# Splitting the first pair's input during the early attention steps, and resuming attention five slots later

## The chip, the cores and the metric

The kernel runs on one core of one Trainium2 chip. The metric is the device time of one execution in microseconds (us), the median of several runs. Profiles come from one profiled execution.

## What is computed

Three stages follow each other: attention against pooled keys and values, a mixture of eight experts with all experts used (weights balanced by eight rounds of row and column scaling), and a softplus network. All is float32; x has 2304 tokens of 512 channels.

```python
# attention: q, k, v are (4, 8, 576, 64); keys and values are means of 8 neighbours
k_p = k.reshape(B, H, Sp, 8, D).mean(axis=3)
v_p = v.reshape(B, H, Sp, 8, D).mean(axis=3)
x = softmax(q @ k_p.T / sqrt(D)) @ v_p          # -> (2304, 512)
# experts
P = exp(x @ w_gate - max)
for _ in range(8):
    P /= P.sum(1); P /= P.sum(0); P *= N / E
x = sum(P[:, e] * (relu(x @ w1[e]) @ w2[e]) for e in range(8))
# softplus network
out = softplus(x @ w_in) @ w_out
```

## The kernel before, in words

**The large products.** The tokens are cut into three pairs of token blocks (512, 896 and 896 tokens). For each pair, the expert stage runs 32 sets; a set is 256 hidden units of one expert. Each float32 operand is split into a high and a low part (`hi` is a copy to fp32r on ScalarE, `lo` the difference from it), and a product is three matmuls, hi·hi, hi·lo and lo·hi, for each of two pieces of 128 rows. The first layer of a set (`first_moe`) multiplies two 2 x 2 block matrices with seven products instead of eight: each takes one part of the weights (`A11`, `A12`, `A22` and the sums `S1` to `S4`, made by `sums_w1` on GpSimd and split by `prep_w1`) and one part of x: the blocks `b11`, `b21`, `b22` themselves, and the differences `t1` to `t4`. The differences for pair 0 are made by `t_sums` (line 437) and all seven parts are split by `splits` and `split_x` (lines 448 and 452), on VectorE or, for the numbers in `on_pool`, on GpSimd. TensorE takes the products in the order b11, t2, t1, t4, t3, b21, b22. Between them VectorE adds the results in PSUM (line 586): `u1` after t2 (t3, which accumulates onto the same bank, waits for it), and three sums after t3 (b22, the last product, waits for the second of them). Then come relu and split (lines 521 and 522) and the second layer (`second`: four token tiles for pair 0, tile `py`, added up on VectorE in line 658). The last product (`rest`) is issued behind the first tile of the second layer of the set before.

**The order is written by hand.** Each engine executes its instructions in the order of the program text. After each of the seven products and each of the four second-layer tiles the program calls `hook`, one slot; so a set of pair 0 has 11 slots (7 in the first set, since no second layer runs beside it).

**Attention** has 32 steps, each for 288 queries of a pair of heads. `attn_step(m)` issues: the transpose of the next queries (`channels_first`, TensorE `pq`, ScalarE `qT`), the scores of step m (`softmax`, TensorE `s`, VectorE line 317 and 318), the gate product every fourth step (`pg`), the transposes of the block before (`turn_attn`, `pa`, `aT`), keys for a pooled pair (`keys_first`, `pk`, `kbd`), the exponential (ScalarE line 321), its division (VectorE lines 325 to 327, GpSimd line 328), the product with the values (`mix`, `px`, which writes x), and at some steps the pooling of a pair of heads (`pool_kv`: two reductions on VectorE, lines 269 and 275; on GpSimd for the first four values). Which steps pool is set by the table `pool_at`: 0, 1, 3, 5, 7, 9, 11, 13 and so on to 25. Each needs its keys one step later (`turn_at`). The first ten steps (`AHEAD`) run alone, one after another, at the start. The others run inside slots: `hook` issues one in every fifth slot (2, 7, 12, ...), so step m stands in slot 2 + 5(m - 10), and steps 10 and 11 lie beside the first set.

**After attention** `finish_attention` puts further work into the list `side`, of which each slot takes one entry: the balancing of the weights, then `shares_to_raw` (line 814 on VectorE), which multiplies the results of the first experts of pair 0, kept unweighted until then, by their shares and adds them up.

Of the kernel before, what the change touches and what calls it, by code (L numbers as in the profile page):

```python
# [9 lines left out]
F32 = mybir.dt.float32  # L10
# [9 lines left out]
def attention_moe_softplus_kernel(  # L20
# [20 lines left out]
    HP = H // 2  # L41
    w_in = w_in.bitcast(U32)
    w_out = w_out.bitcast(U32)
    P = 128
# [18 lines left out]
    TP0 = PAIRS[0]  # L63
# [53 lines left out]
    def x_of(pair):  # L117
        return g_t[0][:, :KC * PAIRS[pair]].rearrange("p (c n) -> p c n", c=KC)
# [25 lines left out]
    raw_t = {}  # L144
# [3 lines left out]
    def load_w(which, n):  # L148
        if n >= len(sets):
            return  # L150
        _, kind, _, u = sets[n]
        shape = [P, KC, US] if which == 1 else [P, UC, DM]
        if kind == "moe":
            e, o = divmod(u, UPE)
            o *= US
            src = w1[e][:, o:o + US] if which == 1 else w2[e][o:o + US, :]
            src = src.rearrange("(c p) f -> p c f", p=P)
        else:
            src = (v1 if which == 1 else v2)[u]
        t = rpool.tile(shape, F32, tag=f"w{which}raw", name=f"w{which}raw")  # L160
        nc.sync.dma_start(t, src)
        raw_t[which, n] = t
# [65 lines left out]
    AHEAD = 10  # L228
# [5 lines left out]
    to_turn = []  # L234
# [30 lines left out]
    def pool_kv(i):  # L265
        kt, vt, pool = kv_t.pop(i)
        kp = at_p.tile([SP, 2, D], F32, tag="kp", name="kp", bufs=1)
        vp = at_p.tile([SP, 2, D], F32, tag="vp", name="vp", bufs=NK + 1)
        nc.vector.tensor_reduce(kp, kt.rearrange("p h t d -> p h d t"), axis=AX.X, op=ALU.add)
        if i < HP:  # L270
            pool_add(vt[:, :, 0:4, :], vt[:, :, 0:4, :], vt[:, :, 4:8, :])
            pool_add(vt[:, :, 0:2, :], vt[:, :, 0:2, :], vt[:, :, 2:4, :])
            pool_add(vp, vt[:, :, 0, :], vt[:, :, 1, :])
        else:
            nc.vector.tensor_reduce(vp, vt.rearrange("p h t d -> p h d t"), axis=AX.X, op=ALU.add)
        pooled[i] = kp, vp

        if pool is ld_p or next_kv[0] < 2 * HP:
            load_kv(pool)
# [25 lines left out]
    def softmax(m):  # L305

        ps = bank("s")
        qT = q_t.pop(m)
        kb = kbd[kv_of(m) % NK]
        for j in range(JH):  # L310
            nc.tensor.matmul(ps[:QP, j * 2 * SP:(j + 1) * 2 * SP], qT[:, j * QP:(j + 1) * QP], kb)
        sv = ps[:QP, :G * SP].rearrange("p (g s) -> p g s", g=G)
        pool = at_e if m < AHEAD and m % 3 == 2 else at_p
        mx = at_p.tile([QP, G], F32, tag="mx", name="mx")
        ex = pool.tile([QP, G, SP], F32, tag="ex", name="ex")
        s1 = ps[:QP, G * SP:G * SP + G]
        nc.vector.tensor_reduce(mx, sv, axis=AX.X, op=ALU.max)
        nc.vector.tensor_tensor(ex, sv, mx.unsqueeze(2).to_broadcast([QP, G, SP]), op=ALU.subtract)

        def exp():  # L320
            nc.scalar.activation(ex, ex, AF.Exp)

        def divide():
            sm = at_p.tile([QP, G], F32, tag="sm", name="sm")
            nc.vector.tensor_reduce(s1, ex, axis=AX.X, op=ALU.add)
            nc.vector.tensor_scalar_add(s1, s1, 1e-9)
            nc.vector.reciprocal(sm, s1)
            nc.gpsimd.tensor_tensor(ex, ex, sm.unsqueeze(2).to_broadcast([QP, G, SP]), op=ALU.mult)
            to_turn.append((m, ex))

        return exp, divide

    def turn_attn():
        m, ex = to_turn.pop(0)
        aT = at_p.tile([SP, 2, W], F32, tag="aT", name="aT")
        for h in range(2):
            pa = bank("pa")
            for j in range(JH):
                nc.tensor.transpose(pa[:SP, j * QP:(j + 1) * QP], ex[:, 2 * j + h, :], ident[:QP, :QP])
            nc.scalar.copy(aT[:, h, :], pa[:SP, :W])  # L340
        to_mix.append((m, aT))
# [40 lines left out]
    pool_at = {}  # L382
    for i in range(2, B * HP):
        b, hp = divmod(i, HP)
        pool_at.setdefault(hp - 2 if b == 0 else 2 * HP * b - 5 + 2 * hp, []).append(i)
    turn_at = {}
    for m, l in pool_at.items():
        turn_at.setdefault(m + 1, []).extend(l)
    turn_at.setdefault(0, []).append(1)

    def attn_step(m, early):


        last = STEPS
        if m + 1 < last:
            channels_first(m + 1)
        if m < last:
            exp, divide = softmax(m)
        while to_gate:
            gate()  # L400
        while to_turn:
            turn_attn()
        for i in turn_at.get(m, ()):
            keys_first(i)
        if m < last:
            exp()
            to_divide.append(divide)
        while len(to_divide) > (1 if early else 0):
            to_divide.pop(0)()
        while len(to_mix) > (0 if early or m >= last else 1):  # L410
            mix()
        for i in pool_at.get(m, ()):
            pool_kv(i)

    for i, pool in enumerate((ld_e, ld_e, ld_p, ld_p)):
        load_kv(pool)
# [18 lines left out]
    def t_sums(x, t, on_pool=()):  # L435

        sub = lambda i, o, a, b: (nc.gpsimd if i in on_pool else nc.vector).tensor_tensor(o, a, b, op=ALU.subtract)
        return [
            lambda: sub(0, t(0), block(x, 0, 1), block(x, 0, 0)),
            lambda: sub(2, t(2), block(x, 1, 1), block(x, 0, 1)),  # L440
            lambda: sub(1, t(1), block(x, 1, 1), t(0)),
            lambda: sub(3, t(3), block(x, 1, 0), t(1)),
        ]
# [41 lines left out]
    def splits(kind, x, t, on_pool=(), pair=None):  # L485
        if kind == "moe":
            l = moe_parts(x, t)
        else:
            l = [
                (f"c{c}{j}", x[:, c:c + cs, j * tb:(j + 1) * tb])  # L490
                for cs, tb in (sp_parts(x.shape[2]),) for j in range(x.shape[2] // tb) for c in range(0, KC, cs)
            ]
        return [
            lambda i=i, a=a: split_x(*a, i in on_pool, None if pair is None else xlod[pair][:, i])
            for i, a in enumerate(l)
        ]
# [284 lines left out]
    def hook(light=True):  # L781
        slot[0] += 1
        if attn_m[0] is not None:
            if slot[0] % 5 == 2:
                attn_step(attn_m[0], False)
                attn_m[0] += 1
                if attn_m[0] >= STEPS and not to_turn and not to_mix and not to_gate:
                    attn_m[0] = None
                    finish_attention()
        elif side:  # L790
            x = side.pop(0)
            if x is not None:
                x()
        elif converting[0] is not None and light and "c" in banks:
            converting[0] += 1
            if converting[0] % 3 and next(conversion, 0) == 0:
                converting[0] = None
# [7 lines left out]
    def shares_to_raw(experts):  # L805

        for e in experts:
            for i in range(TP0 // P):
                def add(i=i, e=e):
                    a, s = acc_of(1, i), prob[:, i, e:e + 1]  # L810
                    if e == 0:
                        nc.scalar.activation(a, a, AF.Copy, scale=s)
                    else:
                        nc.vector.scalar_tensor_tensor(a, raw_of(e, i), s, a, op0=ALU.mult, op1=ALU.add)  # L814
                side.extend([add, None, None] if e else [add])

    def load_x(pair):
        o = OFF[pair] - TP0
# [2 lines left out]
    def t_in(g, pair):  # L821
        v = g_t[g][:, :KC * PAIRS[pair]].rearrange("p (q c n) -> p q c n", q=4, c=2)
        return lambda i: v[:, i]


    for m in range(AHEAD):
        attn_step(m, True)
        if m == 4:
            sums_w1(0)
        if m == 6:  # L830
            prep_w1(0)
            load_w(1, 1)
    ectx.close()
    hctx = ExitStack()
    hpool = hctx.enter_context(tc.tile_pool(name="h", bufs=2, side="right"))
    zpool = hctx.enter_context(tc.tile_pool(name="z", bufs=2, side="right"))
    tpool = None


    ta = hpool.tile([P, 2, 2, TP0 // 2], F32, tag="hhi", name="ta")  # L840
    tb = hpool.tile([P, 2, 2, TP0 // 2], F32, tag="hlo", name="tb")
    t0_of = lambda i: (ta, tb)[i // 2][:, i % 2]
    first_sums = t_sums(x_of(0), t0_of, on_pool=(2,))
    first_splits = splits("moe", x_of(0), t0_of, on_pool=(2, 4))
    first_sums[0]()
    first_splits[0]()
    for x in first_sums[1:]:
        x()
    for x in first_splits[1:]:
        x()  # L850


# [24 lines left out]
    for step, (what, n) in enumerate(todo):  # L877
# [4 lines left out]
        elif what == "first":  # L882
            f, kind, pair, u = sets[n]
            nxt = sets[n + 1] if n + 1 < len(sets) else None
            if not n or sets[n - 1][0] != f:
                xs.update(xs_next)
                xs_next.clear()
            if nxt is not None and nxt[1] == "moe":
                sums_w1(n + 1)
            if nxt is not None and nxt[0] != f:  # L890

# [114 lines left out]
```

## Time and profile before

| | before |
|---|---|
| runs | 2066.97, 2070.39, 2071.49 us; median 2070.39 |
| profiled execution | 2070.89 us, its span 2069.1 us |
| TensorE busy | 2020.9 us, 98% |
| VectorE, ScalarE, GpSimd busy | 1446.9, 829.4, 1242.5 us |
| TensorE's mean granted clock | 0.990 |

The rows further down are of the profiled execution, in us from the start of its span. PE is TensorE, DVE VectorE, ACT ScalarE, POOL GpSimd. A row of a timeline is one instruction or a run of equal ones: start, duration, engine, line, what it writes and reads; in brackets the idle time of the engine before it and what ended that. PEclk is the clock that TensorE was granted as a share of full speed: 0.50 is the lower of its two levels (1.2 GHz), 1.00 the upper (2.4 GHz).

### The profile page before, as it was taken

How to read it: one execution, taken by the hardware profiler on the slowest of the kernel's cores; microseconds unless marked ns; L12 is line 12 of the kernel's file. 1: busy time of each engine (PE TensorE's matmuls, PEld its weight loads, DVE VectorE, ACT ScalarE, POOL GpSimd, SP SyncE). 2: the span in 40 equal slices, each digit the busy share in tenths (PEclk: the TensorE clock that was granted, in tenths of full speed). 3: DMA queues.
4: the chain of work that ended last, by engine and by line, in shares of the span. 5: the costliest groups of instructions: out<-in, count | busy, mean ns of one | idle time of the engine just before them, and what ended most of it. 6: DMA issues, size and time to landing. Idle time of an engine off the chain costs nothing.

```text
span 2069.1 us, 27593 instructions
## 1 busy us (share of the span) xinstructions
PE 2020.9 (98%) x10285; PEld 1745.6 (84%) x10285; DVE 1446.9 (70%) x2467; ACT 829.4 (40%) x1567; POOL 1242.5 (60%) x995
## 2 busy tenths in 40 slices
PE   7899999999999999999999999999999999999998
PEld 5677888888888888888888888888888888888887
DVE  7787587776677777767776776777655666767756
ACT  4555544354322332222243223222222365565554
POOL 4666689987566645556565555665555554544555
PEclk9799999999999999999999999999999999999999
DMA  6343223444223332222242222222211111121132
GB/s 183 87 142 108 87 92 107 149 145 165 85 92 109 93 102 82 90 92 82 87 152 84 72 87 77 92 88 76 74 54 62 62 53 50 62 87 52 62 117 72
DMA packets 133762, 192.00 MB, mean 93 GB/s; under 512 B 26924, under 2 KB 82940, under 8 KB 133628
## 3 DMA queue, kind: packets, MB, share of 16 engines
q1 hardware_dynamic: 133628, 190.25, 29.3%
q8 instruction: 80, 1.31, 0.3%
q14 instruction: 54, 0.44, 0.1%
HBM read 166.94 MB, written 23.27 MB: 92 GB/s over the span
## 4 chain that ended last, share of the span: by engine, by line
PE 80%; POOL 3%; DVE 2%; ACT 1%; DMA 1%; issue 1%; POOLq 0%; SPq 0%; DVEq 0%; ACTq 0%
PE py L506 41%; PE p L506 29%; PE ph L506 9%; POOL w1lo L168 1%; POOL w2lo L168 1%; DMA xlod<-xl 1%; DMA g<-xd 0%; PE pt L668 0%; ACT xhi L448 0%; DVE g L814 0%; ACT w1hi L199 0%; POOL sums L168 0%; DMA f<-in_moe_w_in_dram 0%; DVE g L662 0%; DVE c L537 0%
## 5 line engine op out<-in xcount | busy, mean ns | idle before, releaser
L506 PE MATMUL py<-w2hi,hhi 128*128 128x512 f32 x1440 | 567.6, 394 | 6.1 <-DVE g L662 3.3
L506 PE MATMUL py<-w2hi,hlo 128*128 128x512 f32 x1440 | 562.9, 391 | 0.8 <-POOL hlo L549 0.8
L506 PE MATMUL py<-w2lo,hhi 128*128 128x512 f32 x1440 | 562.4, 391 | 0.0
L168 POOL TENSOR_TENSOR w1lo<-w1raw,w1hi 128x512 fp32r<-128x512 f32 (+1 forms) x216 | 254.0, 1194 | 476.4 <-ACT w1hi L199 375.8
L506 PE MATMUL p<-xhi,w1hi 128*128 128x448 f32 (+1 forms) x1344 | 459.9, 342 | 12.1 <-DVE p L586 4.3
L506 PE MATMUL p<-xhi,w1lo 128*128 128x448 f32 (+1 forms) x1344 | 456.7, 340 | 4.6 <-POOL w1lo L168 4.6
L506 PE MATMUL p<-xlo,w1hi 128*128 128x448 f32 (+1 forms) x1344 | 457.0, 340 | 2.8 <-DVE xlo L452 2.6
L662 DVE SCALAR_TENSOR_TENSOR g<-py,prob,g 128x512 f32<-128x512 f32 x482 | 360.5, 749 | 99.7 <-PE py L506 87.6
L521 ACT ACTIVATE hhi<-p 128x448 fp32r<-128x448 f32 (+1 forms) x384 | 180.1, 494 | 422.8 <-PE p L506 407.5
L506 PEld LDWEIGHTS py<-w2hi,hhi 128*128 128x128 f32 x1440 | 271.1, 188 | 66.4 <-DVE g L662 4.0
L506 PEld LDWEIGHTS py<-w2hi,hlo 128*128 128x128 f32 x1440 | 271.0, 188 | 60.8 <-POOL hlo L549 1.7
L168 POOL TENSOR_TENSOR w2lo<-w2raw,w2hi 128x1024 fp32r<-128x1024 f32 x120 | 288.8, 2406 | 49.6 <-ACT w2hi L212 44.4
L506 PEld LDWEIGHTS py<-w2lo,hhi 128*128 128x128 f32 x1440 | 271.2, 188 | 50.1
L506 PEld LDWEIGHTS p<-xhi,w1hi 128*128 128x128 f32 x1344 | 256.1, 191 | 42.1 <-DVE p L586 5.8
L506 PEld LDWEIGHTS p<-xlo,w1hi 128*128 128x128 f32 x1344 | 256.1, 191 | 21.9 <-DVE xlo L452 3.4
L506 PEld LDWEIGHTS p<-xhi,w1lo 128*128 128x128 f32 x1344 | 256.2, 191 | 18.7 <-POOL w1lo L168 5.9
L588 ACT COPY za<-p 128x448 f32<-128x448 f32 (+1 forms) x96 | 46.0, 479 | 492.4 <-PE p L506 488.1
L168 POOL TENSOR_TENSOR w1lo<-sums,w1hi 128x1024 fp32r<-128x1024 f32 x96 | 231.9, 2416 | 0.0
L522 DVE SCALAR_TENSOR_TENSOR hlo<-p,hhi 128x448 fp32r<-128x448 f32 (+1 forms) x384 | 210.3, 549 | 25.1 <-ACT hhi L521 24.4
L586 DVE TENSOR_TENSOR za<-p,za 128x448 f32<-128x448 f32 (+1 forms) x96 | 53.4, 556 | 166.1 <-PE p L506 166.1
L549 POOL TENSOR_TENSOR hlo<-ln,hhi 128x448 fp32r<-128x448 f32 (+1 forms) x80 | 97.2, 1217 | 51.5 <-ACT hhi L548 51.2
L212 ACT CAST w2hi<-w2raw 128x1024 fp32r<-128x1024 f32 x120 | 126.2, 1052 | 0.0
(124 smaller groups left out, 2618.2 us busy)
## 6 DMA issues: line engine op xcount, KB each, us to landing
w1raw<-in_moe_w_dram SPq DMA_DIRECT2D x96, 512.0 KB
w2raw<-in_moe_w_dram SPq DMA_DIRECT2D x96, 512.0 KB
w1raw<-v SPq DMA_DIRECT2D x24, 512.0 KB
w2raw<-v SPq DMA_DIRECT2D x24, 512.0 KB
f<-in_moe_w_in_dram SPq DMA_DIRECT2D x16, 512.0 KB
v<-dt SPq DMA_DIRECT2D x32, 256.0 KB
f<-in_moe_w_out_dram SPq DMA_DIRECT2D x16, 512.0 KB
xlod<-xl SPq DMA_DIRECT2D x28, 224.0 KB
```

What stands on the lines that cost most here:

```text
L168: nc.gpsimd.tensor_tensor(o, a, b, op=ALU.subtract)
L212: nc.scalar.copy(hi, raw)
L506: nc.tensor.matmul(ps, lhs[a], rhs[b], start=first and i == 0, stop=last and i == 2, skip_group_check=goes_on,)
L521: nc.scalar.activation(hh, src, AF.Relu)
L522: nc.vector.scalar_tensor_tensor(hl, src, 0.0, hh.bitcast(F32), op0=ALU.max, op1=ALU.subtract)
L549: nc.gpsimd.tensor_tensor(hl, l, hh.bitcast(F32), op=ALU.subtract)
L586: add = lambda o, x, y: nc.vector.tensor_tensor(o, x, y, op=ALU.add)
L588: nc.scalar.copy(a, pa)
L662: nc.vector.scalar_tensor_tensor(a, py, prob[:, t, e:e + 1], a, op0=ALU.mult, op1=ALU.add)
```

## The change

Four parts:

1. The parts of pair 0 are made in the early steps where they can be: `b11` is split after step 6, `b21` after step 7, `t1` made and split after step 8; the other three differences and four splits come after step 9, in another order. Three of the subtractions (b11, t1, b21) and that of t3 go to GpSimd (before: t1 and t3). The differences lie in `g1` instead of in tiles of the `h` pool. The split of the first set's weights, and the load of the second set's, come after step 5 instead of 6, the sums of the second set's weights after step 8.
2. The pooling that stood in step 9 (the fourth pair of heads of its batch) moves to step 10, and its keys get a slot of their own.
3. Step 10 runs in slot 7 instead of 2, so step m stands in slot 2 + 5(m - 9). It first turns the block that is waiting.
4. `shares_to_raw` takes two slots for each addition instead of three; the buffers `ex` of steps 1, 4, 7 instead of 2, 5, 8 lie in the early pool.

```diff
-        pool = at_e if m < AHEAD and m % 3 == 2 else at_p
+        pool = at_e if m < AHEAD and m % 3 == 1 else at_p
@@ the table of pooling steps
-        pool_at.setdefault(hp - 2 if b == 0 else 2 * HP * b - 5 + 2 * hp, []).append(i)
+        at = hp - 2 if b == 0 else 2 * HP * b - 5 + 2 * hp
+        pool_at.setdefault(AHEAD if at == AHEAD - 1 else at, []).append(i)
+
+    to_key = []
     turn_at = {}
     for m, l in pool_at.items():
-        turn_at.setdefault(m + 1, []).extend(l)
+        if m != AHEAD:
+            turn_at.setdefault(m + 1, []).extend(l)
@@ attn_step
+        if m == AHEAD:
+            while to_turn:
+                turn_attn()
...
         for i in pool_at.get(m, ()):
             pool_kv(i)
+            if m == AHEAD:
+                to_key.append(i)
@@ hook
-            if slot[0] % 5 == 2:
+            if to_key and slot[0] % 5 == 1:
+                keys_first(to_key.pop(0))
+            if slot[0] > 5 and slot[0] % 5 == 2:
                 attn_step(attn_m[0], False)
@@ shares_to_raw
-                side.extend([add, None, None] if e else [add])
+                side.extend([add, None] if e else [add])
@@ the early steps
+    t0_of = t_in(1, 0)
+    sum1, sum3, sum2, sum4 = t_sums(x_of(0), t0_of, on_pool=(2,))
+    split_b11, split_t2, split_t1, split_t4, split_t3, split_b21, split_b22 = splits(
+        "moe", x_of(0), t0_of, on_pool=(0, 2, 4, 5)
+    )
     for m in range(AHEAD):
         attn_step(m, True)
         if m == 4:
             sums_w1(0)
-        if m == 6:
+        if m == 5:
             prep_w1(0)
             load_w(1, 1)
+        if m == 6:
+            split_b11()
+        if m == 7:
+            split_b21()
+        if m == 8:
+            sum1()
+            split_t1()
+            sums_w1(1)
...
-    ta = hpool.tile([P, 2, 2, TP0 // 2], F32, tag="hhi", name="ta")
-    tb = hpool.tile([P, 2, 2, TP0 // 2], F32, tag="hlo", name="tb")
-    t0_of = lambda i: (ta, tb)[i // 2][:, i % 2]
-    first_sums = t_sums(x_of(0), t0_of, on_pool=(2,))
-    first_splits = splits("moe", x_of(0), t0_of, on_pool=(2, 4))
-    first_sums[0]()
-    first_splits[0]()
-    for x in first_sums[1:]:
-        x()
-    for x in first_splits[1:]:
+    for x in (sum2, split_t2, sum3, sum4, split_t4, split_t3, split_b22):
         x()
@@ the first layer of a set
-            if nxt is not None and nxt[1] == "moe":
+            if nxt is not None and nxt[1] == "moe" and ("s", n + 1) not in raw_t:
                 sums_w1(n + 1)
```

The lines of VectorE's and GpSimd's instructions below are nine higher in the changed kernel where they lie behind the new ones (586 is 595, 658 is 667, 452 is 461, 437 is 446).

**VectorE, the attention step in slot 22** (the fourth slot of the third set), before: step 14. `p_1135` is the bank of t2 and t3, `p_1136` that of t1 and b22.

```order
L317 TENSOR_REDUCE mx<-s 96x6
L318 TENSOR_TENSOR ex<-s,mx 96x432
L299 TENSOR_SCALAR kbd_130<-pk 64x72 x2
L325 TENSOR_REDUCE s<-ex 96x6
L326 TENSOR_SCALAR s<-s 96x6
L327 RECIPROCAL sm<-s 96x6
L586 TENSOR_TENSOR za<-p_1135,za 128x256
L586 TENSOR_TENSOR p_1135<-p_1136,za 128x256
L586 TENSOR_TENSOR p_1137<-p_1137,za 128x256
L522 SCALAR_TENSOR_TENSOR hlo<-p_1134,hhi 128x256
L658 TENSOR_TENSOR g_93<-py,g_93 128x512
L586 TENSOR_TENSOR p_1136<-p_1136,u_1139 128x256
```

The same slot with the change: step 13.

```order
L317 TENSOR_REDUCE mx<-s 96x6
L318 TENSOR_TENSOR ex<-s,mx 96x432
L325 TENSOR_REDUCE s<-ex 96x6
L326 TENSOR_SCALAR s<-s 96x6
L327 RECIPROCAL sm<-s 96x6
L269 TENSOR_REDUCE kp<-kt 72x128
L275 TENSOR_REDUCE vp<-vt 72x128
L595 TENSOR_TENSOR za<-p_1086,za 128x256
L595 TENSOR_TENSOR p_1086<-p_1087,za 128x256
L595 TENSOR_TENSOR p_1088<-p_1088,za 128x256
```

The two reductions of the pooling stand between the softmax and the three sums; before, the slot had a key copy (`kbd`) and no pooling.

**VectorE, the attention step in slot 52** (the first slot of a set), before: step 20.

```order
L317 TENSOR_REDUCE mx<-s 96x6
L318 TENSOR_TENSOR ex<-s,mx 96x432
L299 TENSOR_SCALAR kbd_128<-pk 64x72 x2
L325 TENSOR_REDUCE s<-ex 96x6
L326 TENSOR_SCALAR s<-s 96x6
L327 RECIPROCAL sm<-s 96x6
L586 TENSOR_TENSOR u_1803<-p_1799,za 128x256
L586 TENSOR_TENSOR za<-p_1799,za 128x256
```

The same slot with the change: step 19.

```order
L317 TENSOR_REDUCE mx<-s 96x6
L318 TENSOR_TENSOR ex<-s,mx 96x432
L325 TENSOR_REDUCE s<-ex 96x6
L326 TENSOR_SCALAR s<-s 96x6
L327 RECIPROCAL sm<-s 96x6
L269 TENSOR_REDUCE kp<-kt 72x128
L275 TENSOR_REDUCE vp<-vt 72x128
L595 TENSOR_TENSOR u_1755<-p_1751,za 128x256
L595 TENSOR_TENSOR za<-p_1751,za 128x256
```

Here the reductions stand ahead of `u`.

**GpSimd, from the products of the early steps to the weight sums of the second set**, before (`g_92` holds x, `ta` and `tb` the differences):

```order
L328 TENSOR_TENSOR ex<-ex,sm 96x432 x3
L437 TENSOR_TENSOR tb<-g_92 128x512
L452 TENSOR_TENSOR xlo<-ta,xhi 128x512
L452 TENSOR_TENSOR xlo<-tb,xhi 128x512
L165 TENSOR_TENSOR sums<-w1raw 128x256
L168 TENSOR_TENSOR sums<-w1raw 128x256
L168 TENSOR_TENSOR sums<-sums,w1raw 128x256
L168 TENSOR_TENSOR sums<-w1raw,sums 128x256
```

With the change (`g_93` holds the differences), steps 6 to 9:

```order
L328 TENSOR_TENSOR ex<-ex,sm 96x432
L461 TENSOR_TENSOR xlo<-g_92,xhi 128x512
L328 TENSOR_TENSOR ex<-ex,sm 96x432
L461 TENSOR_TENSOR xlo<-g_92,xhi 128x512
L328 TENSOR_TENSOR ex<-ex,sm 96x432
L461 TENSOR_TENSOR xlo<-g_93,xhi 128x512
L165 TENSOR_TENSOR sums<-w1raw 128x256
L168 TENSOR_TENSOR sums<-w1raw 128x256
L168 TENSOR_TENSOR sums<-sums,w1raw 128x256
L168 TENSOR_TENSOR sums<-w1raw,sums 128x256
L328 TENSOR_TENSOR ex<-ex,sm 96x432
L446 TENSOR_TENSOR g_93<-g_92 128x512
```

A subtraction for x now stands behind each of three products, and the weight sums ahead of the product of step 8.

## Rows read from the trace of the kernel before

**Rows 1.** Page, section 1 (busy time, share, instructions) and section 2 (tenths in 40 slices).

```profile
PE 2020.9 (98%) x10285; PEld 1745.6 (84%) x10285; DVE 1446.9 (70%) x2467; ACT 829.4 (40%) x1567; POOL 1242.5 (60%) x995
...
PEclk9799999999999999999999999999999999999999
```

**Rows 2.** Timeline of TensorE, 48 to 86 us (start us, us, instruction, idle before and releaser).

```profile
48.31 0.74 PE L288 MATMUL pq<-ident,qt 96*128 96x96 f32 x3
...
51.51 1.65 PE L349 MATMUL px<-aT,vp 72*64 72x288 f32 x4
...
57.63 0.58 PE L506 MATMUL p<-xlo,w1hi 128*128 128x256 f32 x1 [2.64 <-DVE xlo L452]
58.01 0.41 PE L506 MATMUL p<-xhi,w1lo 128*128 128x256 f32 x1
58.22 0.41 PE L506 MATMUL p<-xhi,w1hi 128*128 128x256 f32 x1
...
70.09 0.41 PE L288 MATMUL pq<-ident,qt 96*128 96x96 f32 x3
70.34 0.90 PE L311 MATMUL s<-kbd,qT 128*96 128x144 f32 x6
...
74.23 0.39 PE L506 MATMUL p<-xhi,w1hi 128*128 128x256 f32 x1
...
80.75 0.58 PE L506 MATMUL p<-xhi,w1lo 128*128 128x256 f32 x1 [1.38 <-POOL w1lo L168]
...
85.62 0.68 PE L288 MATMUL pq<-ident,qt 96*128 96x96 f32 x3
```

**Rows 3.** Timelines of ScalarE, VectorE and GpSimd, 48 to 64 us.

```profile
53.20 0.36 ACT L357 ACTIVATE g<-px 128x224 f32<-128x224 f32 x1 [0.76 <-PE px L349]
...
53.74 0.62 ACT L448 CAST xhi<-g 128x512 fp32r<-128x512 f32 x1
...
56.30 0.67 DVE L437 TENSOR_TENSOR ta<-g 128x512 f32<-128x512 f32 x1
...
61.19 2.90 DVE L452 TENSOR_TENSOR xlo<-g,xhi 128x512 fp32r<-128x512 f32 x2
...
48.42 0.91 POOL L328 TENSOR_TENSOR ex<-ex,sm 96x432 f32<-96x432 f32 x1 [2.98 <-PE px L349]
```

**Rows 4.** Stretches: us, busy (x) of PE, PEld, DVE, ACT, POOL, PEclk, DMA share, GB/s.

```profile
41.50:53.00 11.50, 10.73 (x43) 7.07 (x43) 8.51 (x16) 5.39 (x14) 4.89 (x6) 0.53 0.51 137
58.00:69.30 11.30, 9.92 (x78) 8.80 (x77) 9.34 (x17) 5.80 (x15) 7.93 (x8) 0.65 0.13 38
77.70:86.00 8.30, 6.89 (x31) 6.60 (x32) 3.62 (x8) 1.37 (x5) 7.37 (x6) 0.50 0.67 199
195.00:200.00 5.00, 5.00 (x31) 4.14 (x35) 2.91 (x8) 2.03 (x4) 3.15 (x2) 0.66 0.24 85
```

**Rows 5.** Timelines of TensorE, then VectorE, step 25 (slot 77), 186 to 195 us.

```profile
186.30 0.41 PE L288 MATMUL pq<-ident,qt 96*128 96x96 f32 x3
...
188.51 0.39 PE L506 MATMUL p<-xhi,w1hi 128*128 128x256 f32 x1
...
190.03 0.40 PE L506 MATMUL py<-w2hi,hhi 128*128 128x512 f32 x1
...
195.00 0.38 PE L506 MATMUL p<-xhi,w1hi 128*128 128x256 f32 x1 [3.42 <-DVE p L586]
...
190.38 1.97 DVE L269 TENSOR_REDUCE kp<-kt 72x128 f32<-72x1024 f32 x1
192.27 1.88 DVE L275 TENSOR_REDUCE vp<-vt 72x128 f32<-72x1024 f32 x1
194.07 0.41 DVE L586 TENSOR_TENSOR za<-p,za 128x256 f32<-128x256 f32 x1
```

**Rows 6.** Timeline of TensorE, step 20 (slot 52).

```profile
154.06 0.39 PE L506 MATMUL p<-xhi,w1hi 128*128 128x256 f32 x1 [1.08 <-DVE u L586]
```

**Rows 7.** Instructions of line 814: duration ns min/median/max, first and last start us.

```profile
L814 DVE SCALAR_TENSOR_TENSOR g<-g,prob,g x13: 740/1255/2445, 322.5 to 370.4; 128x512 f32<-128x512 f32 x13
```

## The prediction

> **What bounds the kernel now.** I read the page first. TensorE is busy for 2020.9 of 2069.1 us [rows 1], so nearly all that can be won is in the 48 us where it waits, and in stretches where it runs at its lower level. The strip of its clock is below 9 in the second of 40 slices alone (51.7 to 103 us), and all that the change moves lies in the first 20% of the span. Next I read TensorE's timeline there. The last early attention step ends at 51.51 + 1.65 = 53.2 us; then TensorE waits, 2.64 us of it for one low half of x [rows 2], because the sums and splits of x begin only now: VectorE's first difference starts at 56.30, after the two reductions of a pooled pair [rows 3]. Later, the first two sets wait for low halves of weights; the last of these waits ends at 80.75, and the slot in which attention step 12 stands starts at 85.62 [rows 2]. The granted clock was 0.53, 0.65 and 0.50 in three stretches of these 45 us [rows 4]. Third, I looked for waits while attention runs beside the first pair, since the change moves all those steps. One stands out: 3.42 us before 195.00, for a sum of VectorE [rows 5].
>
> That wait is the key to the change. Step 25 starts on TensorE at 186.30. VectorE gets its softmax, then the two reductions that pool a pair: 190.38 to about 194.1. Behind them in its queue stand the three sums that the last product of the set needs (`rest`, on `b22`). TensorE has only `t3`, `b21` and one tile of the second layer to do meanwhile [rows 5]. Step 20 shows the same in small without pooling: a wait of 1.08 us for `u1` [rows 6].
>
> **The slots.** A set of pair 0 has 11 slots: k = 0 to 6 in its products, then 4 between the second layer's tiles. A step comes every 5 slots, a pooling step every 10, so the place of pooling in the set goes back by one with each. Counted from the program, before: steps 13, 15, ..., 25 pool at slots 17, 27, ..., 77, which are second-layer places 2, 1, 0, then k = 6, 5, 4, 3. Only the last, step 25 at k = 3, stands where sums follow closely. Five slots later, the same steps pool at slots 22, 32, 42, 52, 62, 72, 82: k = 3, 2, 1, 0, then second-layer places 3, 2, 1. The steps that don't pool take the harmless places. The order of the instructions agrees: pooling now stands directly ahead of the sums in steps 13, 15 and 17, and ahead of `u1` in 19 and 21.
>
> **Price of the pooling steps.** Take step 25 as the pattern (no gate, nothing left over from before) [rows 5]. From the start of a step to its end TensorE works 188.51 - 186.30 = 2.2 us, a product is (190.03 - 188.51)/2 = 0.76 with the first one's restart, say 0.72; the sum that `rest` needs comes 195.00 - 186.30 = 8.7 us after the step's start, `u1` (which would stand where `za` does at 194.07) about 8.2 us after it.
> - Step 13 (k = 3): the place of step 25, so 3.4 us.
> - Step 15 (k = 2): one product more as cover: 3.4 - 0.7 = 2.7 us.
> - Step 17 (k = 1): after its four products step 18 follows before `rest`, another 1.6 us and more of cover: no wait.
> - Step 19 (k = 0): TensorE needs `u1` after 2.2 + 3 x 0.72 = 4.4 us, and gets it at 8.2: 3.8 us.
> - Step 21 (last tile's place): four products, 2.2 + 2.9 = 5.1 us: 3.1 us.
> - Steps 23 and 25 have a tile or two and another step ahead of `u1`: no wait, as with 13 and 15 before.
>
> That is 13.0 us of new waits. Gone are the 3.42 us (slot 77 now holds step 24, which doesn't pool) and the 1.08 us (slot 52 is counted anew above): net **+8.5 us**. Bounds: +5 if each cover is 0.9 us longer than I count, and +9.6 if the 1.08 us comes on top.
>
> **The clock.** After the 3.42 us the granted clock over 195 to 200 was 0.66 [rows 4], which is 5 x 0.34 = 1.7 us lost; after 1.08 us nothing fell. Four waits of 2.7 to 3.8 us, all nearer to 3.42 than to 1.08, instead of one: 3 x 1.7 = **+5.1 us**; bounds 0 and 5.1. The Trainium skill, TensorE: Matmul & The Clock Gate, section HAM oscillation — how this bites in real kernels, speaks against the change in this way too: a wait ahead of every block of matmuls brings the lower level back each time. [...]
>
> **The early part.** Before, from 53.2 to 85.62 is 32.4 us, of which attention step 11 takes 74.23 - 70.09 = 4.1 [rows 2]; it is now done a step later, at the same price. So 28.3 us are to be compared. After, `b11` is split long before, and the pair's pooling (3.8 us on VectorE) no longer stands in front. TensorE starts at 53.2. At the low level a product is 6 x 0.21 = 1.3 us, from the steps of its matmuls [rows 2]. `t2` needs the last channels of x (copied by 53.56), a difference (0.67), a cast (0.62) and a subtraction, as long as the difference [rows 3], so 55.5; one of them may be held up by GpSimd, which costs 0.78: two subtractions took 2.90 instead of 1.34 beside it [rows 3]. `t2` then ends at 56.3 + 1.1 = 57.4. `t1`, `t4`, `t3`, `b21` follow without a wait: 2.9 us at full clock, 5.1 at half. Step 10 up to the end of its scores: 3.2 us at half clock (48.31 to 51.51 are the same pieces of step 9), some 1.6 at full [rows 2]. So the scores end between 61.9 and 65.7. From there the old chain holds, since the change leaves it: softmax, the copy and cast behind it, then the low halves of the second set's weights on GpSimd, which stand behind that step's product. In step 11 the scores ended at 70.34 + 0.90 = 71.2 and the last weight wait at 80.75: 9.5 us. Then 4.9 us to the slot of step 12. After: 76.3 to 80.1, or 23.1 to 26.9 us against 28.3: a gain of 1.4 to 5.2. Step 11 turned two blocks of attention ahead of that chain, step 10 turns one, so I take a value in the upper half, **-4 us**. Bounds: 0 (all five of VectorE's operations held up), and -8 with the low stretch 77.7 to 86 (8.3 us at 0.50, worth half of its 6.89 busy us [rows 4]) gone too.
>
> **What I cost at nothing.** The three splits, three subtractions of some 1.3 us and the second set's weight sums, now on GpSimd between steps 6 and 9: GpSimd idled for 2.98 us ahead of its product in step 8 [rows 3], and that of step 9 is needed in step 10 only. If that cover is gone, each of the three steps is 1.3 us longer. The weight load that comes one step sooner: its data are used 10 us later. Keys later by a step: one transpose in its own slot. The expert adds after attention, one in two slots instead of three: 13 of them took 740 to 2445 ns, median 1255 [rows 7], so 12 of them in 24 slots keep VectorE full for two sets; TensorE waited for none of them before. Bounds -1 and +3, taken as 0.
>
> **Sum.** -4 + 8.5 + 5.1 = +9.6 us. The profiled execution took 2070.9 us (span 2069.1), 0.5 above the median 2070.4; on the median this gives **2080 us**.
>
> **The rivals.**
> - *Operations of VectorE blocked throughout the start.* GpSimd's queue is now full from step 8 on (a subtraction, four weight sums, a product, a difference, a subtraction), and VectorE's five operations run beside it. 5 x 0.78 = 3.9 us eat the early gain: 2070.9 + 13.6 = 2084.5. The Trainium skill, SBUF — State Buffer, section Who interferes with whom, has this as a rule: a VectorE operation with two inputs in SBUF waits for a GpSimd one that reads SBUF, for its whole length. The 2.90 us agree. For it: the rows. Against it: VectorE got its turn between two operations of GpSimd there, so a wait is a part of one of these and not the row. Chance 0.2. In this case the change does not do what it says: x is split early, but not ready early.
> - *No difference.* The start gains the bound of 8, and the waits bring no lower clock: 2070.9 - 8 + 8.5 = 2071.4. For it: the weight waits and 8.3 us at 0.50 are there to be won. Against it: these hang on the attention step ahead, which stays. Chance 0.14.
> - *Faster: the clock stays up.* Starting without the gap of 53 to 58, TensorE would hold full clock from 41 us on. It decides if the granted clock is 1.00 through steps 8 and 9 as well. Worth half of the low share: 10.73 x 0.47 + 9.92 x 0.35 + 6.89 x 0.50 = 12.0 us [rows 4], and 4 us of waits; with 8.5 of new waits and no lower clock after them: 2070.9 - 16 + 8.5 = 2063.4. For it: in 58 to 69.3 us the clock was partly back already, 0.65 on the mean. Against it: in 41 to 53 TensorE was busy for 10.73 of 11.5 us and still had 0.53. Chance 0.16.
> - My forecast: 0.5.
>
> **How the numbers follow.** A measurement of this kernel can tell about 0.2%, 4 us, from no change. The forecast and the first rival are slower by more (0.7), the second is the same (0.14), the third faster (0.16). The range goes from the third rival's edge, 2064, to the first with the expert adds' upper bound, 2088. The likeliest case alone: 2075 to 2084.
>
> **What would show it.** Right: waits of 2.5 to 4 us on TensorE for the sums or `u1` in steps 13, 15, 19 and 21, none at 24, a low clock after each; `b11` without a wait right after the last early step, a first wait of at most 3 us for `t2`; two weight waits after step 10. Wrong: none of the four waits (then VectorE was ahead, and the time is below 2070), or full clock from 58 to 90 us.

## The result, and the profile after

The changed kernel takes **2083.15 us** (median of 4 runs, 2080.80 to 2086.52); the kernel before, on the same chip, 2070.66 us. The ratio is 1.0060, with a 95% interval of 1.0048 to 1.0073: slower by 10 to 15 us. The forecast was 2080, slower.

The page of the kernel after, sections 1 and 2, the rows that answer to [rows 1]:

```profile
PE 2019.4 (97%) x10285; PEld 1746.3 (84%) x10285; DVE 1449.2 (70%) x2465; ACT 829.8 (40%) x1567; POOL 1245.3 (60%) x997
...
PEclk9899999999999999999999999999999999999999
```

TensorE is no busier than before and the strip of its clock is a tenth better in one slice: whole-span rows don't show where 12 us went. The waits do. These are the waits of over 2 us in TensorE's timeline of the kernel after, 100 to 190 us, and VectorE's timeline ahead of the first of them:

```profile
105.65 0.58 PE L515 MATMUL p<-xhi,w1hi 128*128 128x256 f32 x1 [3.42 <-DVE p L595]
127.16 0.39 PE L515 MATMUL p<-xhi,w1hi 128*128 128x256 f32 x1 [2.75 <-DVE p L595]
161.69 0.39 PE L515 MATMUL p<-xhi,w1hi 128*128 128x256 f32 x1 [3.54 <-DVE u L595]
181.89 0.38 PE L515 MATMUL p<-xhi,w1hi 128*128 128x256 f32 x1 [2.86 <-DVE u L595]
...
100.92 0.19 DVE L327 RECIPROCAL sm<-s 96x6 f32<-96x6 f32 x1
101.04 1.96 DVE L269 TENSOR_REDUCE kp<-kt 72x128 f32<-72x1024 f32 x1
102.92 1.88 DVE L275 TENSOR_REDUCE vp<-vt 72x128 f32<-72x1024 f32 x1
104.72 0.41 DVE L595 TENSOR_TENSOR za<-p,za 128x256 f32<-128x256 f32 x1
105.17 0.76 DVE L595 TENSOR_TENSOR p<-p,za 128x256 f32<-128x256 f32 x2
```

These are steps 13, 15, 19 and 21, and no other: step 17 brings no wait of over 0.4 us, step 24 in slot 77 none. In step 13 the sums stand behind both reductions in VectorE's queue, as they did in step 25 before [rows 5]. The stretches behind the four waits (columns as in [rows 4]):

```profile
105.65:112.00 6.35, 6.35 (x53) 5.44 (x53) 3.41 (x8) 2.04 (x4) 3.15 (x2) 0.57 0.66 165
126.00:132.00 6.00, 4.84 (x27) 3.92 (x28) 4.68 (x13) 2.14 (x6) 2.32 (x1) 0.72 0.67 200
161.00:167.00 6.00, 5.09 (x30) 4.83 (x32) 2.73 (x7) 1.09 (x3) 0.00 (x0) 0.72 0.39 112
181.00:187.00 6.00, 4.96 (x54) 4.11 (x54) 3.23 (x7) 1.49 (x6) 0.72 (x1) 0.72 0.67 182
```

The clock fell behind each. The start, in TensorE's, VectorE's and GpSimd's timelines after, then two stretches:

```profile
52.40 0.69 PE L339 MATMUL pa<-ident,ex 96*72 96x96 f32 x6 [3.10 <-POOL ex L328]
53.38 1.52 PE L349 MATMUL px<-aT,vp 72*64 72x288 f32 x4 [0.29 <-ACT aT L340]
54.83 0.58 PE L515 MATMUL p<-xhi,w1hi 128*128 128x256 f32 x1
...
59.45 0.58 PE L515 MATMUL p<-xlo,w1hi 128*128 128x256 f32 x1 [1.99 <-DVE xlo L461]
...
65.89 0.98 PE L311 MATMUL s<-kbd,qT 128*96 128x144 f32 x6
69.86 0.39 PE L515 MATMUL p<-xhi,w1hi 128*128 128x256 f32 x1 [1.47 <-ACT w1hi L199]
72.43 0.39 PE L515 MATMUL p<-xhi,w1lo 128*128 128x256 f32 x1 [2.07 <-POOL w1lo L168]
75.44 0.58 PE L515 MATMUL p<-xhi,w1lo 128*128 128x256 f32 x1 [2.03 <-POOL w1lo L168]
80.48 0.41 PE L288 MATMUL pq<-ident,qt 96*128 96x96 f32 x3
...
56.86 2.54 DVE L461 TENSOR_TENSOR xlo<-g,xhi 128x512 fp32r<-128x512 f32 x1 [0.68 <-ACT xhi L457]
...
55.71 1.06 POOL L168 TENSOR_TENSOR sums<-w1raw,sums 128x256 f32<-128x256 f32 x1
56.73 0.90 POOL L328 TENSOR_TENSOR ex<-ex,sm 96x432 f32<-96x432 f32 x1
57.59 1.26 POOL L446 TENSOR_TENSOR g<-g 128x512 f32<-128x512 f32 x1
...
41.50:53.00 11.50, 7.54 (x50) 5.25 (x48) 10.01 (x18) 5.87 (x17) 5.22 (x5) 0.94 0.36 92
53.00:58.00 5.00, 3.77 (x13) 2.22 (x11) 2.67 (x5) 2.37 (x6) 4.92 (x7) 0.51 0.13 30
```

`b11` starts without a wait (54.83), but `t2` waits again, for one subtraction of 2.54 us beside GpSimd's operations, and there are three waits for weights behind step 10 (1.47, 2.07 and 2.03 us). The slot of step 12 starts at 80.48; before it was 85.62, of which 4.14 were step 11: counted from the start of the span, 1.0 us is won. The early steps themselves end 1.7 us later than before (53.38 + 1.52 = 54.90, before 53.16), with a wait of 3.10 us for the product of step 8; from their end to the slot of step 12 it is 25.6 us, before 28.3.

**The ledger.** The loads of `w2raw` come once for each set, so their starts in SP's timeline tell how far two kernels are apart at each place. After less before, in us, at load 3 (about 110 us; kernels that resume at slot 7 have then done one step less, worth 4.1 us), 8 (poolings over, 200 us), 16 (end of attention, 310), 26 (end of the expert adds, 424) and 60 (993). The rows below the first belong to the runs that follow.

| kernel | 3 | 8 | 16 | 26 | 60 |
|---|---|---|---|---|---|
| after | -4.3 | +13.9 | +11.8 | +13.1 | +12.9 |
| old slots | +3.5 | +3.5 | +4.6 | +6.4 | +12.6 |
| poolings moved | -4.0 | -4.4 | -6.8 | -5.5 | -5.7 |
| spare products | -3.5 | +8.2 | +6.1 | +7.5 | +7.4 |
| old slots and adds | +2.6 | +2.6 | +2.5 | +2.5 | +2.7 |
| adds alone undone | -5.6 | +11.9 | +9.8 | +9.2 | +9.2 |
| x late | -5.3 | +12.0 | +9.5 | +10.8 | +11.0 |
| sums later | -6.8 | +11.8 | +9.7 | +11.0 | +13.9 |
| weights sooner | -6.6 | +10.5 | +8.4 | +9.7 | +12.7 |
| all together | -10.1 | -10.6 | -12.9 | -13.5 | -13.0 |

The early steps, alike in the changed kernel and in six of these runs, end up to 2 us apart from one execution to the next (53.7 to 55.8 us), so a difference below that in the column of load 3 says nothing. Of the 12.9 us, 11.8 are there when attention ends, 1.3 come with the expert adds, nothing later. (The spans of the two profiles differ by 10.9 only: before, the granted clock was 0.84 over the last 9 us, which is 1.4 of the 2 us between the two figures; after, it was 1.00.)

### The profile page after: what moved, and what is told of

The parts are those of the page before. It is cut to its first block, busy times and chain, and to the rows that moved or that the text cites. A ratio compares the mean times of both kernels' runs of the same rounds, so it can differ in the third digit from the quotient of the medians.

```text
span 2080.0 us, 27588 instructions
## 1 busy us (share of the span) xinstructions
PE 2019.4 (97%) x10285; PEld 1746.3 (84%) x10285; DVE 1449.2 (70%) x2465; ACT 829.8 (40%) x1567; POOL 1245.3 (60%) x997
## 4 chain that ended last, share of the span: by engine, by line
PE 88%; DVE 6%; POOL 2%; ACT 2%; DMA 1%; issue 1%; SPq 0%; POOLq 0%; DVEq 0%; ACTq 0%
PE py L515 44%; PE p L515 31%; PE ph L515 9%; POOL w1lo L168 1%; PE s L311 1%; PE px L349 1%; DVE kp L269 1%; DMA xlod<-xl 1%; DVE vp L275 1%; PE pa L339 0%; POOL w2lo L168 0%; DVE g L825 0%; DMA g<-xd 0%; ACT xhi L457 0%; PE pt L677 0%
## 5 line engine op out<-in xcount | busy, mean ns | idle before, releaser
L515 PE MATMUL p<-xhi,w1hi 128*128 128x448 f32 (+1 forms) x1344 | 460.4, 343 | 22.1 <-DVE u L595 11.7
```

Of the source, the lines that this page charges most:

```text
L515: nc.tensor.matmul(ps, lhs[a], rhs[b], start=first and i == 0, stop=last and i == 2, skip_group_check=goes_on,)
```

## The experiments

**One part undone: the slots.**

```diff
-            if slot[0] > 5 and slot[0] % 5 == 2:
+            if slot[0] % 5 == 2:
```

> The changed kernel with its third part alone undone: attention resumes at the second slot again, so that steps 13 to 25 pool in the slots in which they pooled before the change; x is still split early, the expert adds still come every other slot. Theory A (the loss is four waits behind poolings, in steps 13, 15, 19 and 21, and the lower clock after each): the four waits are gone, the 3.4 us of step 25 and about 1 us of step 20 are back; 2067 to 2072 us. Theory B (the loss is in the start, where GpSimd's splits and sums hold VectorE up): it stays, 2080 to 2084. Theory C (the loss is in the expert adds, which come every other slot): it stays, about 2082.

Measured: 2083.27 us, ratio 1.0066 (1.0053 to 1.0078). By the time alone theory A has fallen; the trace says otherwise. Between loads 3 and 8 the ledger stands still at +3.5: none of the four waits is there, and TensorE waits for sums of VectorE as it did before. The kernel lost the same amount at other places: 3.5 us by load 3, 2.9 between loads 8 and 26, and 6.2 between loads 26 and 60. Timelines of this run, SP, VectorE and TensorE:

```profile
430.82 0.37 SPq L161 DMA_DIRECT2D w2raw<-in_moe_w_dram  x1
431.24 8.01 SPq L485 DMA_DIRECT2D xlod<-xl  x3
...
428.75 0.61 DVE L484 TENSOR_TENSOR xl<-g,xh 128x448 fp32r<-128x448 f32 x1
429.32 0.42 DVE L595 TENSOR_TENSOR u<-p,za 128x256 f32<-128x256 f32 x1
435.64 0.62 DVE L484 TENSOR_TENSOR xl<-g,xh 128x448 fp32r<-128x448 f32 x1 [5.89 <-DMA xlod<-xl]
...
437.11 0.58 PE L515 MATMUL p<-xhi,w1hi 128*128 128x256 f32 x1 [3.63 <-DVE p L595]
```

Low halves of the next pair's x are written to memory; the writes stand in SP's queue behind a load of `w2raw` (430.82), for which SP waits 5.1 us on GpSimd's `w2lo`. VectorE stands 5.89 us for the buffer, and TensorE 3.63 us behind it; over 436 to 450 us the granted clock is 0.88.

**The same, and the expert adds as before** (`[add, None]` back to `[add, None, None]`).

> The first run with the old slots, and the expert adds back in every third slot: of the change there remain the early splits of x and pair 7 pooled a step later. In the first run the four waits were gone, but 3.6 us were lost in the start, 2.2 in the adds stage, and some 6 between 430 and 470 us, where VectorE stood for 5.9 us at a low half of the next pair's x for a buffer that a transfer still read. Theory F (the 6 and the 2.2 us come from the place of the adds, that is from when the next pair's sums and low halves meet the transfers): both go, 3 to 4 us remain: 2073 to 2075 us. Rival: they come from the splits or the slots: 2081 or more.

Measured: 2073.45 us, 1.0016 (1.0007 to 1.0025). The losses after load 3 are gone, as theory F has it. So without the slots and the adds 2 to 3 us are left of the loss; the ledger has them at load 3 already, where differences up to 2 us say nothing, so their place is not shown. And one edit, the adds, is worth 10 us here.

**The adds alone undone.**

> The changed kernel with the expert adds back in every third slot alone. Theory A puts 1.2 us on them (the three waits for u of 1.07, 1.49 and 1.04 us in 330 to 360 us): those waits go, 2081 to 2083 us, if nothing collides between 430 and 470 us. Theory C (the loss is in the adds): about 2071. Theory F (their place decides what collides later): waits of several us between 430 and 470 us may come or not, 2081 to 2089.

Measured: 2081.49 us, 1.0049 (1.0034 to 1.0064). Between loads 16 and 26, where the changed kernel lost 1.3 us, this one gains 0.6, so 1.9 in the ledger; the ratios differ by 0.0011, 2.3 us, within their intervals. The same edit that costs 10 us with the old slots costs about 2 here. VectorE's waits for the writes of the next pair's x are at most 3.06 us in the changed kernel and 3.23 in this run, as they were before (2.94); with the old slots two were 5.89 and 4.18. Why they grow there was not tried. Theory C falls.

**The poolings moved out of the four places.**

```diff
+        if 9 <= i <= 14:
+            at -= 1
         pool_at.setdefault(AHEAD if at == AHEAD - 1 else at, []).append(i)
```

> The changed kernel with the poolings of pairs 9 to 14 one attention step sooner (steps 12, 14, ..., 22 in place of 13, 15, ..., 23): they fall into slots behind which TensorE has three or more products or tiles and another step ahead of a sum. Nothing else moves. Theory A: the waits of 3.4, 2.75, 3.5 and 2.9 us and the lower clock after each go (12.6 + 4 x 1.6 = 19 us); what may come is a wait of about 1 us in slot 52, where a step without pooling stands: 2064 to 2066 us, below both kernels. Theories B and C: within 2 us of the changed kernel, 2081 to 2085.

Measured: 2064.77 us, 0.9978 (0.9969 to 0.9987). The costliest TensorE group in 98 to 200 us (line, tile, count, busy, mean ns, idle before and releasers), after:

```profile
L515 PE MATMUL p<-xhi,w1hi 128*128 128x256 f32 x70 | 21.4, 305 | 12.6 <-DVE u L595 6.4 <-DVE p L595 6.2
```

and with the poolings moved:

```profile
L517 PE MATMUL p<-xhi,w1hi 128*128 128x256 f32 x82 | 24.1, 293 | 1.1 <-DVE u L597 0.9 <-DVE p L597 0.2
```

12.6 us of waits became 1.1, and the kernel is 18.4 us faster than the changed one by the medians, 17.0 by the ratios: the waits and what the clock adds. That is theory A in the kernel where it matters.

**Waits filled with spare products**, to tell waits from clock. `spin` multiplies a block of weights by `b11` into a bank that nobody reads; it stands ahead of the last product (sets 2 and 3) and of `t3` (sets 5 and 6).

```diff
+        fill = {2: (4, 0), 3: (3, 0), 5: (0, 4), 6: (0, 3)}.get(n, (0, 0))
...
+        spin(fill[1])
         product(pb, S3, "t3", True)
...
         def rest():
+            spin(fill[0])
             product(pc, S4, "b22", True)
```

> The changed kernel with spare products on TensorE (of a block of weights and b11, into a bank that nobody reads) where the four waits are: four ahead of the last product of the set in step 13, three in step 15, four ahead of t3 in step 19, three in step 21, each some 0.7 us, 10 of the 12.6 us. The sums come as late as before, so the waits cost what they cost, but TensorE has work. It adds work and leaves none out. Theory A with the clock as its second term: the granted clock stays at 0.95 or more behind all four, 2083.2 - 4 x 1.6 = 2077 us. If the clock falls for another reason than the idle time: 2083. If the spare work itself runs late and pushes the set back: above 2083.

Measured: 2077.95 us, 1.0038 (1.0025 to 1.0051). Timeline of this run around the first wait, and the stretches around all four:

```profile
105.48 0.28 PE L515 MATMUL d<-xhi,w1lo 128*128 128x256 f32 x1
106.49 0.39 PE L515 MATMUL p<-xhi,w1hi 128*128 128x256 f32 x1 [0.73 <-DVE p L595]
...
100.00:112.00 12.00, 11.27 (x107) 9.68 (x107) 10.26 (x19) 6.47 (x16) 7.59 (x5) 1.00 0.49 149
122.00:134.00 12.00, 11.27 (x75) 9.62 (x74) 10.58 (x21) 5.49 (x13) 7.58 (x6) 1.00 0.37 107
155.00:167.00 12.00, 10.95 (x78) 9.53 (x77) 8.58 (x16) 5.11 (x12) 5.04 (x7) 1.00 0.43 119
175.00:187.00 12.00, 10.64 (x99) 8.77 (x99) 8.46 (x18) 6.66 (x17) 5.78 (x8) 1.00 0.50 145
```

The sums come as late as before (14 spare products of 0.7 us and the 3.1 us of waits that are left fill the 12.6 us), but the clock is 1.00 where it was 0.57 and 0.72. The work that TensorE does in those microseconds is thrown away, and still 5.2 us come back (4.6 by the ratios, 5.7 in the ledger at load 8): this is the clock's share, by itself.

**One wait alone, in the kernel before** (the last pair pooled in step 24 in place of step 25).

> The kernel before the change with one pooling moved, that of the last pair, from step 25 (slot 77, k = 3) to step 24 (slot 72, behind the third tile of the second layer). It prices one wait by itself. Theory A: the 3.42 us and the 1.7 us at the lower clock behind it go, 2070.7 - 5.1 = 2065.6 us. If the clock falls there for another reason: 2067.3. If the wait only changes its place (VectorE late wherever it pools): 2070.7.

Measured: 2067.05 us, 0.9990 (0.9981 to 0.9999): 2 to 3 us, not 5. TensorE's timeline of this run:

```profile
190.01 0.39 PE L506 MATMUL p<-xhi,w1hi 128*128 128x256 f32 x1 [0.84 <-DVE u L586]
193.67 0.39 PE L506 MATMUL p<-xhi,w1hi 128*128 128x256 f32 x1 [0.58 <-DVE p L586]
```

The 3.42 us and the lower clock are gone, as expected (1.00 over 186 to 200 us), but waits of 0.84 and 0.58 us came, which I had not counted: slot 72 is not free of cost, slot 77 with a step without pooling neither. The profiled execution was the slowest of twelve, 2071.29 us: by the ledger it is 3.0 us ahead of the kernel before at load 16, and only 0.5 at load 60.

**The start: x late, sums later, weights sooner.** The first puts all splits behind the last early step again; the second removes one line; the third moves a call.

```diff
             split_t1()
-            sums_w1(1)
```

```diff
             def between(k):
+                if n == 0 and k == 0:
+                    prep_w1(1)
+                    load_w(1, 2)
```

> The changed kernel with its first part alone undone: all differences and splits of x begin behind the last early step, as before the change, and the weight sums of the second set behind them. It prices the early splits. By the ledger of the two traces (slot of step 12 one microsecond sooner, step 11 counted apart): 2083 to 2085 us. If the early splits were worth the 4 us of the forecast and something else took 3 us: 2087. If they cost something, as GpSimd's queue could have it: below 2082.

> The changed kernel with the four weight sums of the second set taken out of GpSimd's queue at step 8 and put behind all splits, where GpSimd idles. In the changed kernel VectorE's subtraction for t2 took 2.54 us at 56.86, while GpSimd ran sums and a difference back to back from 53.54 to 58.85. Theory D (VectorE is held up by GpSimd's operations beside it): that subtraction takes 0.7 to 1.3 us, t2's wait falls from 1.99 us to 0.8 or less, and load 10 of w2 comes 1 to 2 us sooner; 2081 to 2082 us. Rival E (what x gains, the low halves of the second set's weights take back): t2's wait falls, but the three weight waits grow by as much; 2083. If the subtraction stays at 2.5 us, D is wrong.

> The changed kernel with the second set's weights split and reduced to low halves ahead of step 10 (between the first product and the second), while GpSimd idles for 6.78 us ahead of step 10's product; before, they stand behind that step's product. Theory E (the early part is bounded by that chain, so that splitting x sooner hardly helps): the waits of 1.47, 2.07 and 2.03 us after step 10 go, 5.6 us, and up to 2 us at the lower clock: 2075.5 to 2078 us. Rival: step 10's softmax or the reductions of the pair pooled there come late next, and half or more of it is back as a wait for them: 2080 or more.

Measured: x late 2080.72 us, 1.0057 (1.0041 to 1.0074); sums later 2083.64, 1.0064 (1.0049 to 1.0079); weights sooner 2082.15, 1.0049 (1.0032 to 1.0066). None differs from the changed kernel's 1.0060 by more than the intervals. So the early splits, the first part of the change, buy nothing that can be measured. The median of x late, 2080.72, lies where its expectation has the splits cost something, but the ratios are only 0.0003 apart, so a cost is not shown either. The traces tell why. TensorE's with x late:

```profile
52.34 1.65 PE L349 MATMUL px<-aT,vp 72*64 72x288 f32 x4
55.24 0.58 PE L515 MATMUL p<-xhi,w1hi 128*128 128x256 f32 x1 [1.25 <-ACT xhi L457]
56.33 0.58 PE L515 MATMUL p<-xlo,w1hi 128*128 128x256 f32 x1 [0.51 <-DVE xlo L461]
...
79.57 0.41 PE L288 MATMUL pq<-ident,qt 96*128 96x96 f32 x3
```

From the end of the last early step (53.99) to the slot of step 12 it is 25.6 us, as in the changed kernel: x split late costs waits of 1.25 and 0.51 us and 1.11 for `u1`, x split early 0.40 and 1.99, and the last wait for weights is 1.37 us with x late, 2.03 in the changed kernel. So the gain over the 28.3 us of before is there without the early splits. In both kernels the reductions of a pooled pair, 3.8 us of VectorE, no longer stand ahead of the sums of x; that this is what brings it was not tried by itself. With the sums later, VectorE's and GpSimd's rows:

```profile
54.52 0.99 DVE L461 TENSOR_TENSOR xlo<-g,xhi 128x512 fp32r<-128x512 f32 x1 [0.68 <-ACT xhi L457]
...
53.19 1.77 POOL L446 TENSOR_TENSOR g<-g 128x512 f32<-128x512 f32 x1
```

The subtraction takes 0.99 in place of 2.54 and the wait of `t2` falls from 1.99 to 0.64 us, so theory D is right about the mechanism. It is not right about the time: from the end of the early steps (52.72) to the slot of step 12 (78.04) it is 25.3 us, since a wait for a cast grew from 0.40 to 0.92 and one of 0.59 for `u1` came in. With the weights sooner, TensorE's:

```profile
74.13 0.28 PE L297 MATMUL pk<-ident,kp 72*128 72x72 f32 x1 [2.86 <-DVE hlo L531]
75.78 0.45 PE L515 MATMUL p<-xhi,w1hi 128*128 128x256 f32 x1 [1.37 <-DVE u L595]
```

The three waits for weights are gone, and 2.86 + 1.37 us for VectorE came, which reduces pair 7 just then: the rival. From the early steps' end (55.05) to the slot of step 12 (77.11) it is 22.1 us, 3.5 less than in the changed kernel. At load 8 the two are ahead by 2.1 and 3.4 us. With the sums later this is no gain of the edit: its early steps ended 2.2 us sooner (52.72 for 54.90), ahead of where the sums stood (53.54). Both leads were lost later: 2.9 and 3.0 us between loads 26 and 60. There the clock fell in both where it had not in the changed kernel: 0.88 over 436 to 450 us, 0.93 over 515 to 540. TensorE's wait in the first of these stretches and the stretch, in the changed kernel:

```profile
444.08 0.50 PE L515 MATMUL py<-w2hi,hhi 128*128 128x512 f32 x1 [1.78 <-DVE g L671]
...
436.00:450.00 14.00, 12.22 (x80) 10.83 (x79) 8.65 (x19) 6.50 (x14) 13.61 (x13) 1.00 0.54 153
```

and in the run with the sums later:

```profile
441.98 0.50 PE L515 MATMUL py<-w2hi,hhi 128*128 128x512 f32 x1 [1.77 <-DVE g L671]
...
436.00:450.00 14.00, 12.23 (x67) 10.42 (x66) 7.76 (x16) 6.40 (x13) 11.71 (x12) 0.88 0.51 179
```

14 us at 0.88 are 1.7 us, and 25 us at 0.93 another 1.7: together as much as or more than the two runs were ahead.

**Versions that beat both.** Poolings moved and the adds every third slot; then also the weight sums later and the weights sooner.

> The poolings moved (as in the second run) and the expert adds in every third slot. If the two terms add up: 2064.8 less the 1.7 us that the adds alone gave, 2063 us. If moving the adds makes low halves of the next pair's x meet their transfers: 2066 to 2070.

> All that gave something in a trace, together: poolings moved, expert adds in every third slot, weight sums of the second set behind the splits, that set's weights split ahead of step 10. If the gains of the traces add up (18.4, 1.7, 2.1, 3.4 from 2083.2): 2057.6 us. If the clock takes the two early gains back later, as it did in the runs that had them alone: 2061 to 2064.

Measured: 2062.25 us, 0.9963 (0.9950 to 0.9976); and **2059.69 us, 0.9949** (0.9934 to 0.9964), 9.7 us faster than the kernel before and 23 faster than the changed one. The two terms of the first add up. The second lies between its two expectations, 2.6 us below the first, so the early gains are kept in part (by the traces, that of the weights; the sums later gave none). It still has 2.86 and 1.37 us of waits for VectorE in step 10.

## Why the prediction was right, and where it was not

- **Pooling waits, +8.5 net: right.** 3.42 + 2.75 + 3.54 + 2.86 = 12.57 us against 13.0, at the four places named, none elsewhere; less 3.42 and 1.08, net 8.1. The pattern of step 25 carried it. That the poolings are the cause is shown by moving them (12.6 us of waits to 1.1, 17 to 18 us less).
- **Clock, +5.1: right.** All four waits brought the lower level; filling them gave back 5.2 us (4.6 by the ratios), for four. What the ledger leaves for the clock, 11.8 + 1.0 - 8.1 = 4.7 net of the one that went, agrees. The Trainium skill, TensorE: Matmul & The Clock Gate, section HAM oscillation — how this bites in real kernels, shows a kernel in which the wait ahead of each block of matmuls brings the lower level back every time. The trace agrees for these four; the waits of that kernel are longer than 2.75 and 2.86 us, so for these two the trace alone speaks.
- **Early part, -4: wrong in size, and the splits are not what gave it.** Counted as in the forecast, from the end of the last early step to the slot of step 12, the gain is 28.3 - 25.6 = 2.7 us, inside the bounds but in their lower half; 1.0 of it is left from the start of the span, and 1.7, the later end of the early steps, is within what they vary by. With x late the same stretch is 25.6 us too. Two steps failed. "One of them may be held up by GpSimd, which costs 0.78": it cost 2.54 - 0.67 = 1.87, because the subtraction got no turn between GpSimd's product and its difference and ended 0.55 us after the difference (58.85). So the argument against the first rival was wrong for this operation; the other four took 0.68 to 1.35, which is why the rival as a whole did not come. The Trainium skill, SBUF — State Buffer, section Who interferes with whom, has a VectorE instruction with two inputs in SBUF contend with a GpSimd instruction that reads SBUF, by an exclusive lock. The trace agrees: with the sums later the same subtraction again ended 0.55 us after GpSimd's difference (55.51 and 54.96). And the upper half was taken for the gain: the scores ended 12.0 us after the early steps, at the late end of the 8.7 to 12.5 forecast. "From there the old chain holds" was right: 8.6 us to the last weight wait, for 9.5, then 5.0 for 4.9.
- **Expert adds, 0: wrong by about 1.3 us**, through waits for `u`: 1.07, 1.49 and 1.04 us in 330 to 360 us, where before there was one of 0.61. The bound of +3 held them here, but not with the old slots, where the same edit cost 10 us. I had looked at the adds' own cover alone, not at what starts when they end.
- **The sum** came to +9.6, the ledger to +12.9: the early part 3 too good and the adds 1.3 too good, waits and clock 0.8 too dear together. The range held it.
- The third rival (full clock from the start) did not come, but half of its sign did: the granted clock over 41.5 to 53 us was 0.94, before 0.53. It won nothing, since TensorE then waited 3.10 us for the product of step 8, and over 53 to 58 us the clock was 0.51. With x late it was 0.93 in the same stretch, so the early splits did not raise it.

## What to carry to other kernels

When work is moved by whole slots, write out in which place of the inner cycle each heavy piece lands, and take the price of a bad place from the one instance that the trace already has; a table that moves the pieces by one step may then be worth more than the change under study. Price a wait of TensorE together with the clock behind it, which here added some 1.3 to 1.8 us to each wait of about 3 us (5.2 us for four when they were filled; 18.6 - 11.5 = 7.1 in the ledger at load 16 when the poolings moved). When one part is undone and the time does not move, compare the two traces place by place before the theory is dropped: here two equal times were made of different losses. Count a stretch from where it starts in that execution, too: the steps ahead of it varied by 2 us.

## What was not expected

- The same wait, 1.78 and 1.77 us, was followed by the full clock in one kernel and by 14 us at 0.88 in another. Leads of 2 to 3 us were given back that way 380 us later. What decides it was not tried. One of the four executions with the weights sooner took 2077.66 us at a mean granted clock of 0.993 (the others 2081.66 to 2082.93 at 0.989 or 0.990), which would fit one without that fall; there is no trace of it.
- Products whose result nobody reads made the kernel 5 us faster.
- A side task that runs every other slot instead of every third cost about 2 us with the slots of the change, and 10 us with the old ones, where it starts five slots sooner.
